# A backward pass of two attention blocks on one core: the second half of q by tokens made during the core loop, and o leaving PSUM by one copy

## The chip, the cores and the metric

The kernel runs on one core of one Trainium2 chip. A core has a matrix engine (TensorE, PE in the profile; its weight loads are PEld), VectorE (DVE), ScalarE (ACT), GpSimd (POOL) and SyncE (SP), which here only issues transfers; 16 DMA engines serve all of them. The metric is the time of one execution on the device in microseconds (us), as the median of several runs.

## The reference

Forward outputs and all gradients are computed in one launch, in bf16, for two attention blocks side by side: block A (linear attention with a feature map) and block B (16 query heads that share one key and one value head, softmax). Sequence length 2048, model width 448, head size 28. The change touches block B alone:

```python
def _B_ref(x, wq, wk, wv, wo):
    B, S, D = x.shape
    H = 16
    Dh = D // H
    q = (x @ wq).reshape(B, S, H, Dh).transpose(0, 2, 1, 3)
    k = x @ wk
    v = x @ wv
    scores = einsum("bhqd,bkd->bhqk", q, k) * (Dh ** -0.5)
    p = softmax(scores, axis=-1)
    o = einsum("bhqk,bkd->bhqd", p, v)
    return o.transpose(0, 2, 1, 3).reshape(B, S, H * Dh) @ wo

out, vjp = jax.vjp(f, A_x, A_wqkv, A_wo, B_x, B_wq, B_wk, B_wv, B_wo)
grads = vjp(grad_out)
```

## The kernel before

The program has three stages. Block A takes the first 190 us. A short stage, `phase_B_pre`, makes q, k and v of block B from about 192 to 221 us. The core, the loop over `u`, makes block B's attention forward and backward at once until about 1030 us, and a tail makes the last weight and input gradients.

**`phase_B_pre`.** For each of 4 groups of 512 tokens (`qc`) it makes q with its channels on the partitions, in `qT` (`R1`): heads are padded to 32 channels, 4 heads to a 128-row slab `g`. Row 0 of each head gets a shift for the softmax, written by four small GpSimd transfers (L580). The core also needs q with its tokens on the rows, in `qn_d` in HBM. After groups 1 and 3, four transposes (L585, by DMA, on SyncE's queue) turn 1024 tokens into `gaT`, and one transfer (L586) stores 1 MB of it.

**The core.** There are 64 blocks `b`, each of 256 queries and two heads, and 8 units `u` to a block, so 512 units; one unit is 256 keys. The order on every engine is written out by hand (`tc.manual_schedule()`). A unit of the stream contains:

- TensorE: the scores S of unit `u` into two of three PSUM banks `SB` (`sps`), and dP = v do of unit `u - 16` into the two banks `DB` (`dps`); in even units o and dq of four earlier units (`o_dq`, into `oq`) and dv (`dv_mm`, into `dv_acc`); in odd units dk (`dk_m`, into `dk_acc`).
- ScalarE: two exponentials, `eT` (L891 and L931), and between them a copy of one half of dP, `cp` (L898).
- VectorE: one half of dS, `dsT` (L896), and a 32 x 32 transpose of an earlier `dsT`, `dsx` (L962).
- GpSimd: the other half of dS (L899).
- SyncE: after every fourth unit one DMA transpose of four units of `eT` into `eN` (L933), 1 MB, which `dv_mm` reads.

Once in a block of 8 units the finished o is handled. At unit 8b + 9, VectorE copies it from `oq` into `oTs` (L913). At 8b + 10, TensorE transposes it with an identity matrix (`onat_T`) into a bank called `spare`, which is the bank of the first S product of the next unit. VectorE then reads it in `o_norm`: the reciprocal of the softmax sum (channel 0, L782) and the scaled o into `oTs` (L783). GpSimd follows with the elementwise product of o and do (`prod`, L787), do divided by the sum (`don`, L790), and a copy of the scaled o over do in `do_nat` (L791). At 8b + 12, `row_D` sums `prod` on VectorE (L795) and GpSimd puts the result into channel 0 of `don` (L796). At 8b + 14, TensorE transposes `don` (`don_T`, L804), which becomes the operand of dP from unit 8b + 16 on.

Every 64 units GpSimd issues the loads of the next `qX` from `qn_d` (L904), 256 KB each and two at a time, at units 38 and 54 of the 64 (the first ones at 10 and 18). It also issues the stores of the output (L711) and one load `wo` (L907, at unit 44). Up to unit 127, `do_proj` makes do from the output gradient and its copies go through VectorE (L866).

A tile of PSUM that one engine reads can be written by TensorE only after that engine has finished; all such waits are semaphores that the framework sets.

Of the kernel before, what the change touches and what calls it, by code (L numbers as in the profile page):

```python
# [9 lines left out]
ALU = mybir.AluOpType  # L10
AX = mybir.AxisListType
BF16 = mybir.dt.bfloat16
F32 = mybir.dt.float32
# [4 lines left out]
P = 128  # L18
# [6 lines left out]
def kernel(  # L25
# [21 lines left out]
    nc = tc.nc  # L47
# [21 lines left out]
    qn_d = dpool.tile([S, 512], BF16, name="qn_d")  # L69
# [9 lines left out]
    def mm(out_ap, lhsT, rhs, start=True, stop=True):  # L79
        nc.tensor.matmul(out_ap, lhsT=lhsT, rhs=rhs, start=start, stop=stop, tile_position=(0, 0))  # L80

    def flat(t):
        return t.rearrange("p a b -> p (a b)")
# [430 lines left out]
    def phase_B_pre(pa, cA, awk, psA, io):  # L514
# [3 lines left out]
        def gen(shape, dt=F32):  # L518
            return psA.tile(shape, dt, name="agen")
# [13 lines left out]
        def k_max(qc, sq):  # L533
            ps = gen([H, 512])
            mm(ps[:, :], ones16[0:32, :], sq[0:32, :])
            nc.vector.tensor_reduce(out=kmx[:, qc:qc + 1], in_=ps[:, :], axis=AX.X, op=ALU.max)

        prev = None
        for qc in range(NQC):
            for w, dst in [(0, kT), (1, vT)]:  # L540
# [7 lines left out]
                else:  # L548
# [4 lines left out]
                                    in1=kT[0:32, qc * 512:(qc + 1) * 512], op=ALU.mult)  # L553
# [5 lines left out]
        for qc in range(NQC):  # L559
            qs = slice(qc * 512, (qc + 1) * 512)  # L560
            pn = psA.tile([P, 512], F32, name="aacc")
            sqs = []
            for g in range(6):
                if qc == 0 and g == 2:
                    k_max(NQC - 1, prev)
                    nc.vector.tensor_reduce(out=kmax2[:], in_=kmx[:], axis=AX.X, op=ALU.max)
                if g < 4:
                    ps = gen([P, 512])
                    for c in range(4):
                        mm(ps[:, :], wq_pad[:, c, g * P:(g + 1) * P], xbT[:, c, qs], start=(c == 0), stop=(c == 3))  # L570
                    nc.scalar.activation(out=qT[:, g, qs], in_=ps[:, :], func=ACT.Copy)
                    sq = awk.tile([P, 512], BF16, name="osb")
                    nc.vector.tensor_tensor(out=sq[:, :], in0=qT[:, g, qs], in1=qT[:, g, qs], op=ALU.mult)
                    sqs.append(sq)
                if g >= 2:
                    mm(pn[:, :], bsel[:, g - 2, :], sqs[g - 2][:, :], start=(g == 2), stop=(g == 5))
            shift = shifts[qc]
            nc.scalar.activation(out=shift, in_=pn[0:H, :], func=ACT.Sqrt, scale=kmax2[:, 0:1])
            for g in range(4):
                nc.gpsimd.dma_start(qT[:, g, qs].rearrange("(j r) s -> j r s", r=32)[:, 0, :], shift[4 * g:4 * g + 4, :])  # L580
            if qc % 2:
                q2 = slice((qc - 1) * 512, (qc + 1) * 512)
                t2 = slice(4 * qc - 4, 4 * qc + 4)
                for g in range(4):
                    nc.sync.dma_start_transpose(qn[:, t2, g * P:(g + 1) * P], qT[:, g, q2])  # L585
                nc.sync.dma_start(qn_d[q2, :].rearrange("(t p) c -> p t c", p=P), qn[:, t2, :])  # L586
# [11 lines left out]
    with ExitStack() as pa:  # L598
        psA = pa.enter_context(tc.tile_pool(name="psA", bufs=4, space=bass.MemoryType.PSUM))
        cA = pa.enter_context(tc.tile_pool(name="cA", bufs=1, side="right"))  # L600
        cB = pa.enter_context(tc.tile_pool(name="cB", bufs=1, side="right"))
        awk = pa.enter_context(tc.tile_pool(name="awk", bufs=3, side="right"))
        io = phase_A(pa, cA, cB, awk, psA)
        phase_B_pre(pa, cA, awk, psA, io)
# [3 lines left out]
    qT_B = [R1[:, g, :] for g in range(4)]  # L608
    vaug, kn, do_nat = vaug_, kn_, R2x[:, 0:NS, :]
    psc = ExitStack()  # L610
    with ExitStack() as cs_:
# [8 lines left out]
        pw_ = cs_.enter_context(tc.tile_pool(name="cwk", bufs=4, side="right"))  # L620
        pp_ = cs_.enter_context(tc.tile_pool(name="cout", bufs=2, side="right"))
# [6 lines left out]
        dsT, dsx, qX, don, doT, rl, prod = ({} for _ in range(7))  # L628
# [13 lines left out]
        def blk(b):  # L642
            qc, pair = divmod(b, 8)
            return qc, pair, pair // 2, pair % 2
# [27 lines left out]
        identF = pp_.tile([P, P], F32, name="identF", bufs=1)  # L672
        make_identity(nc, identF[:])
        oTs = pp_.tile([P, 256], F32, name="oTs", bufs=1)
        wo = pc_.tile([P, 4, D], BF16, name="wo", bufs=1)
        oTq = flat(R4).rearrange("p (t k) -> p t k", k=P)
        W4 = D // 4
        outs = {}
        for m in range(2):
            for n in range(15):  # L680
                q_ = n + (n > 13)
                outs[128 * m + 144 + 8 * n] = (4 * m + q_ // 4, q_ % 4 * W4 - (n == 14) * W4, (q_ % 4 + 1) * W4)
        for n in range(7):
            q_ = n + (n > 5)
# [92 lines left out]
        def o_norm(b):  # L777
            onp = onps.pop(b)
            qc, pair, g, hp = blk(b)
            r_ = pw_.tile([P, 2, 2, 1], F32, name="rl")  # L780
            os_ = oTs[:, 0:P].rearrange("p (q h c) -> p q h c", q=2, h=2)
            nc.vector.reciprocal(out=r_[:], in_=onp[:, :, :, 0:1])  # L782
            nc.vector.tensor_tensor(out=os_, in0=onp[:, :, :, :], in1=r_[:].to_broadcast([P, 2, 2, 32]), op=ALU.mult)  # L783
            rl[b] = r_
            dnv = do_nat[:, 2 * qc:2 * qc + 2, pair * 64:pair * 64 + 64].rearrange("p q (h c) -> p q h c", c=32)
            prod[b] = pw_.tile([P, 2, 2, 32], F32, name="prod", bufs=1)
            nc.gpsimd.tensor_tensor(out=prod[b][:], in0=dnv, in1=os_, op=ALU.mult)  # L787
            dn = pw_.tile([P, 2, 2, 32], BF16, name="don", bufs=3)
            don[b] = dn
            nc.gpsimd.tensor_tensor(out=dn[:], in0=dnv, in1=r_[:].to_broadcast([P, 2, 2, 32]), op=ALU.mult)  # L790
            nc.gpsimd.tensor_copy(out=dnv, in_=os_)  # L791

        def row_D(b):
            Dq = pw_.tile([P, 2, 2, 1], F32, name="Dq")
# [74 lines left out]
        with tc.manual_schedule():  # L869
            tc.keep_in_program_order(nc.scalar.activation(out=ex[:], in_=ex[:], func=ACT.Exp))  # L870
            for u in range(NU + 28):
# [28 lines left out]
                for a in {10: (0, 2), 18: (1, 3)}.get(u, ()) or {38: (0, 2), 54: (1, 3)}.get(u % 64, ()) * (u < 448):  # L900
                    qc = u // 64 + (u > 20)
                    if a == 0:
                        qX[qc] = (pqb_ if qc % 2 else pqa_).tile([P, 4, 2, 512], BF16, name="qX")
                    nc.gpsimd.dma_start(qX[qc][32 * a:32 * a + 32, :, :, :].rearrange("j b s c -> j b (s c)"),  # L904
                                        qn_d[qc * 256:(qc + 1) * 256, :].rearrange("(b j s) c -> j b (s c)", b=4, s=2))
                if u == 44:
                    nc.gpsimd.dma_start(wo, wo_d[:, 0:D].rearrange("(g p) c -> p g c", p=P))  # L907
                if (b := due(u, 12)) is not None:
# [5 lines left out]
                if (b := due(u, 27)) is not None:  # L914
                    qc, pair, g, hp = blk(b)
                    nc.vector.tensor_scalar(out=qT_B[g][64 * hp:64 * hp + 64, qc * 256:(qc + 1) * 256],  # L916
                                            in0=oq[64:128, 0:256], scalar1=scale, scalar2=None, op0=ALU.mult)
                if (b := due(u, 10)) is not None:
                    o_norm(b)
                    if b in (15, 31, 47, 55, 63):  # L920
                        t0, t1 = 2 * (b // 8) - 2 * (b < 48), 2 * (b // 8) + 2
                        nc.sync.dma_start_transpose(oTq[:, 4 * (t0 % 4):4 * (t0 % 4) + 4 * (t1 - t0), :],
                                                    do_nat[:, t0:t1, :].rearrange("p q c -> p (q c)"))
# [12 lines left out]
                if u % 2:  # L936
                    b, i = divmod(u - 27, 8)
# [3 lines left out]
                else:  # L941
                    o_dq((u - 2, u - 1), (u - 20, u - 19))
                    b, n = divmod(u - 20, 8)
# [14 lines left out]
                if 0 <= y < NU:  # L958
                    b, tp = divmod(y, 8)
                    if tp == 0:  # L960
                        dsx[b] = px_.tile([P, 8, 2, 2, 256], BF16, name="dsx")
                    nc.vector.transpose(  # L962
                        out=dsx[b][:, tp, :, :, :].rearrange("p h t c -> p (h t c)").bitcast(F32),
                        in_=dsT[y][:, :, :].rearrange("p h c -> p (h c)").bitcast(F32))
# [16 lines left out]
        for c in range(4):  # L981
            t = dkvT[0:32, :].rearrange("p (t a i) -> p t a i", a=4, i=32)[:, :, c, :]
# [83 lines left out]
```

## Time and profile before

| | |
|---|---|
| median of 13 runs | 1087.62 us |
| lowest and highest | 1082.30 and 1097.21 us |
| the profiled execution | 1097.21 us, span of its instructions 1095.5 us |
| granted TensorE clock, mean of the span | 0.99 |
| busy in the span: PE, DVE, ACT, POOL | 95%, 82%, 80%, 70% |
| bytes moved by DMA | 199.24 MB, of which 175.18 MB on q1, the queue of SyncE |

The profiled execution is the slowest of the 13. In a profile, "idle before, releaser" is the time in which the engine stood before an instruction, and the instruction elsewhere that ended it; "issue" means that nothing in the profile explains the wait. Busy times of VectorE and ScalarE overlap a little at the ends of neighbouring instructions, so the distance between two starts is the better measure of their pace.

### The profile page before, as it was taken

The numbers are of one execution on the slowest core, as the hardware profiler recorded it, in microseconds if no ns is written. First come the engines' busy times: TensorE is split into PE (matmuls) and PEld (weight loads), VectorE is DVE, ScalarE is ACT, GpSimd is POOL, SyncE is SP. The second block draws the span as 40 slices with busy tenths as digits, with TensorE's granted clock in tenths as the row PEclk, the third lists the DMA queues.
The fourth block names the chain that finished last, engine by engine and source line by source line (L and its number), as shares of the span: only waits on it lengthen the run. The fifth ranks groups of instructions, "written<-read, shape, count | busy, mean of one in ns | idle before, by whom it ended". The sixth has DMA issues, their size and how long they took to land.

```text
span 1095.5 us, 41904 instructions
## 1 busy us (share of the span) xinstructions
PE 1041.6 (95%) x17241; PEld 504.6 (46%) x17241; DVE 897.7 (82%) x1790; ACT 874.3 (80%) x1744; POOL 761.9 (70%) x993
## 2 busy tenths in 40 slices
PE   9999999999788999999999999999999999999998
PEld 5545555444343444444444444444444444444444
DVE  7896400439787999999999999999999999999842
ACT  6453122579787999999999999999999999999531
POOL 6001242328776888889889888988988898888840
PEclk9999999989899999999999999999999999999999
DMA  9879899299999999999999999999999999999962
GB/s 241 160 132 190 170 192 216 55 218 198 148 153 189 198 193 187 195 174 202 203 177 186 209 199 181 205 184 187 193 205 187 189 193 197 184 175 180 227 139 64
DMA packets 668384, 199.24 MB, mean 182 GB/s; under 512 B 645408, under 2 KB 664144, under 8 KB 668192
## 3 DMA queue, kind: packets, MB, share of 16 engines
q1 hardware_dynamic: 656320, 175.18, 95.7%
q0 software_dynamic: 6912, 17.43, 7.0%
q10 hardware_dynamic: 4960, 3.96, 1.3%
q8 instruction: 135, 2.21, 0.8%
q14 instruction: 57, 0.47, 0.2%
HBM read 21.00 MB, written 12.94 MB: 31 GB/s over the span
## 4 chain that ended last, share of the span: by engine, by line
PE 34%; ACT 24%; issue 17%; DVE 15%; POOL 8%; DMA 1%; DVEq 0%; ACTq 0%; POOLq 0%; SPq 0%
ACT cp L898 13%; ACT eT L931 10%; PE agen L80 8%; PE sps L639 7%; DVE dsx L962 6%; POOL dsT L899 5%; PE aacc L80 4%; PE oq L639 4%; DVE dsT L896 4%; PE sps L80 4%; PE dk_acc L639 2%; DVE oTs L913 2%; PE dps L639 2%; DVE oTs L783 1%; PE dps L80 1%
## 5 line engine op out<-in xcount | busy, mean ns | idle before, releaser
L899 POOL TENSOR_TENSOR dsT<-cp,eT 128x512 bf16<-128x512 bf16 x512 | 589.1, 1158 | 113.8 <-ACT cp L898 106.1
L639 PEld LDWEIGHTS <-R 128*32 128x32 bf16 (+1 forms) x9184 | 238.2, 94 | 283.2 <-issue 247.9
L896 DVE TENSOR_TENSOR dsT<-dps,eT 128x512 bf16<-128x512 f32 x512 | 342.0, 668 | 26.2 <-PE dps L639 20.9
L962 DVE STREAM_TRANSPOSE dsx<-dsT 128x512 f32<-128x512 f32 x512 | 357.7, 699 | 2.4 <-DVE ot L709 0.2
L891 ACT ACTIVATE eT<-sps 128x512 bf16<-128x512 f32 x512 | 312.9, 611 | 36.1 <-PE dps L639 22.1
L898 ACT ACTIVATE cp<-dps 128x512 bf16<-128x512 f32 x512 | 314.5, 614 | 12.0 <-PE dps L639 10.5
L931 ACT ACTIVATE eT<-sps 128x512 bf16<-128x512 f32 x512 | 320.7, 626 | 0.0
L639 PE MATMUL dk_acc<-dsx,qX 32*32 32x512 bf16 x4096 | 270.2, 378 | 3.8 <-issue 3.8
L639 PE MATMUL dps<-doT,R 32*128 32x256 bf16 x2048 | 247.6, 270 | 2.4 <-DVE dsT L896 0.7
L639 PE MATMUL sps<-R,R 32*128 32x256 bf16 (+1 forms) x2240 | 224.0, 276 | 10.4 <-DVE R L866 1.7
L639 PE MATMUL oq<-dsT,R 128*32 128x256 bf16 x2048 | 157.7, 275 | 6.9 <-issue 6.8
L639 PE MATMUL oq<-eT,R 128*32 128x256 bf16 x2048 | 159.3, 276 | 1.0 <-issue 1.0
L639 PEld LDWEIGHTS <-qX 32*32 32x32 bf16 x4096 | 80.2, 89 | 118.9 <-issue 59.1
L639 PE MATMUL dv_acc<-eN,don 128*32 128x512 bf16 x1024 | 98.0, 381 | 0.0
L80 PEld LDWEIGHTS <-R 128*128 128x128 bf16 (+1 forms) x525 | 41.4, 99 | 42.0 <-issue 15.0
L400 POOL COPY pk<-R 128x256 bf16<-128x256 bf16 x4 | 1.6, 398 | 73.8 <-DVE R L360 73.7
L552 DVE TENSOR_TENSOR osb<-R 32x512 bf16<-32x512 bf16 x4 | 1.7, 413 | 59.0 <-ACT R L549 59.0
L639 PE MATMUL sps<-identF,oTs 128*32 128x64 f32 x1024 | 27.9, 225 | 7.9 <-issue 0.4
L639 PEld LDWEIGHTS <-don 128*32 128x32 bf16 x1024 | 34.8, 98 | 0.5
L787 POOL TENSOR_TENSOR prod<-R,oTs 128x128 f32<-128x128 bf16 x64 | 27.7, 433 | 8.2 <-DVE oTs L783 8.2
L916 DVE TENSOR_SCALAR R<-oq 64x256 bf16<-64x256 f32 x64 | 27.3, 427 | 4.4 <-PE oq L639 2.4
L80 PE MATMUL agen<-R,R 128*128 128x448 bf16 x128 | 28.6, 352 | 0.8 <-ACT R L219 0.6
(223 smaller groups left out, 986.8 us busy)
## 6 DMA issues: line engine op xcount, KB each, us to landing
qX<-qn_d POOLq DMA_DIRECT2D x32, 256.0 KB, 4.7
out_dram<-osb ACTq DMA_DIRECT2D x22, 112.0 KB
qn_d<-gaT SPq DMA_DIRECT2D x2, 1024.0 KB
eN<-eT SPq DMA_TRANSPOSE x128
xa<-in_A_x_dram SPq DMA_DIRECT2D x8, 224.0 KB
ga<-in_grad_out_dram SPq DMA_DIRECT2D x4, 448.0 KB
xa<-in_grad_out_dram POOLq DMA_DIRECT2D x4, 448.0 KB, 8.9
out_dram<-wdq POOLq DMA_DIRECT2D x8, 224.0 KB, 4.4
```

The source lines that it names most:

```text
L80: nc.tensor.matmul(out_ap, lhsT=lhsT, rhs=rhs, start=start, stop=stop, tile_position=(0, 0))
L639: nc.tensor.matmul(out, lhsT=lhsT, rhs=rhs, start=start, stop=stop, tile_position=pos, skip_group_check=True)
L783: nc.vector.tensor_tensor(out=os_, in0=onp[:, :, :, :], in1=r_[:].to_broadcast([P, 2, 2, 32]), op=ALU.mult)
L787: nc.gpsimd.tensor_tensor(out=prod[b][:], in0=dnv, in1=os_, op=ALU.mult)
L891: nc.scalar.activation(out=eT(u)[:, 0, :], in_=sp[0][:, :], func=ACT.Exp, scale=scale)
L896: nc.vector.tensor_tensor(out=dst[:, 0, :], in0=dp[0][:, :], in1=ew[:, 0, :], op=ALU.mult)
L898: nc.scalar.activation(out=cp[:, :], in_=dp[1][:, :], func=ACT.Copy)
L899: nc.gpsimd.tensor_tensor(out=dst[:, 1, :], in0=cp[:, :], in1=ew[:, 1, :], op=ALU.mult)
L913: nc.vector.tensor_copy(out=oTs[0:64, :], in_=oq[0:64, 0:256])
L916: nc.vector.tensor_scalar(out=qT_B[g][64 * hp:64 * hp + 64, qc * 256:(qc + 1) * 256], in0=oq[64:128, 0:256], scalar1=scale, scalar2=None, ...
L931: nc.scalar.activation(out=eT(u)[:, 1, :], in_=sp[1][:, :], func=ACT.Exp, scale=scale)
L962: nc.vector.transpose(out=dsx[b][:, tp, :, :, :].rearrange("p h t c -> p (h t c)").bitcast(F32), in_=dsT[y][:, :, :].rearrange("p h c -> p ...
```

## The change

It has two parts. First, `phase_B_pre` makes only the first half of q by tokens (`if qc == 1`). The second half, blocks 4 to 7 of 256 queries, is made during the core: at units 122, 186, 250 and 314 four DMA transposes on SyncE's queue bring one block of 256 tokens into a new tile `qS`, and 10 units later two GpSimd transfers store it in `qn_d`. Second, `o_norm` copies the whole o from PSUM to `oTs` without scaling and takes the reciprocal from that copy. GpSimd now makes `don` first, `prod` from `don` and the unscaled o, and the scaled o for `do_nat` by a product in place of the copy.

```diff
-            if qc % 2:
+            if qc == 1:
                 q2 = slice((qc - 1) * 512, (qc + 1) * 512)
                 t2 = slice(4 * qc - 4, 4 * qc + 4)
                 for g in range(4):
                     nc.sync.dma_start_transpose(qn[:, t2, g * P:(g + 1) * P], qT[:, g, q2])
...
+        qS = pp_.tile([P, 8, P], BF16, name="qS", bufs=1)
...
             os_ = oTs[:, 0:P].rearrange("p (q h c) -> p q h c", q=2, h=2)
-            nc.vector.reciprocal(out=r_[:], in_=onp[:, :, :, 0:1])
-            nc.vector.tensor_tensor(out=os_, in0=onp[:, :, :, :], in1=r_[:].to_broadcast([P, 2, 2, 32]), op=ALU.mult)
+            nc.vector.tensor_copy(out=os_, in_=onp[:, :, :, :])
+            nc.vector.reciprocal(out=r_[:], in_=os_[:, :, :, 0:1])
             rl[b] = r_
             dnv = do_nat[:, 2 * qc:2 * qc + 2, pair * 64:pair * 64 + 64].rearrange("p q (h c) -> p q h c", c=32)
-            prod[b] = pw_.tile([P, 2, 2, 32], F32, name="prod", bufs=1)
-            nc.gpsimd.tensor_tensor(out=prod[b][:], in0=dnv, in1=os_, op=ALU.mult)
             dn = pw_.tile([P, 2, 2, 32], BF16, name="don", bufs=3)
             don[b] = dn
             nc.gpsimd.tensor_tensor(out=dn[:], in0=dnv, in1=r_[:].to_broadcast([P, 2, 2, 32]), op=ALU.mult)
-            nc.gpsimd.tensor_copy(out=dnv, in_=os_)
+            prod[b] = pw_.tile([P, 2, 2, 32], F32, name="prod", bufs=1)
+            nc.gpsimd.tensor_tensor(out=prod[b][:], in0=dn[:], in1=os_, op=ALU.mult)
+            nc.gpsimd.tensor_tensor(out=dnv, in0=os_, in1=r_[:].to_broadcast([P, 2, 2, 32]), op=ALU.mult)
...
+                if u in (122, 186, 250, 314):
+                    q_ = u // 64 + 3
+                    for g_ in range(4):
+                        nc.sync.dma_start_transpose(qS[:, 2 * g_:2 * g_ + 2, :], qT_B[g_][:, q_ * 256:(q_ + 1) * 256])
+                if u in (132, 196, 260, 324):
+                    q_ = u // 64 + 2
+                    for t in range(2):
+                        nc.gpsimd.dma_start(
+                            qn_d[q_ * 256 + t * P:q_ * 256 + (t + 1) * P, :].rearrange("p (g c) -> p g c", c=P),
+                            qS[:, :, :].rearrange("p (g t) c -> p t g c", t=2)[:, t, :, :])
                 if u == 44:
                     nc.gpsimd.dma_start(wo, wo_d[:, 0:D].rearrange("(g p) c -> p g c", p=P))
                 if (b := due(u, 12)) is not None:
                     row_D(b)
```

## The prediction

> **What bounds the kernel now.** I read the windows first (which stretches run off pace), then the SyncE queue and TensorE's waits in the slow ones, then the timelines of one undisturbed block of 8 units. Columns of a window: PE, PEld, DVE, ACT and POOL busy, granted clock, DMA share, GB/s.
>
> ```profile
> 280.00:300.00 20.00, 14.47 (x282) 6.53 (x276) 13.87 (x28) 13.88 (x29) 13.58 (x17) 0.88 1.25 131
> 300.00:320.00 20.00, 17.08 (x320) 7.44 (x312) 15.11 (x28) 15.12 (x31) 13.47 (x16) 0.86 1.27 171
> 320.00:340.00 20.00, 15.77 (x308) 7.16 (x304) 14.66 (x30) 14.52 (x29) 12.34 (x15) 0.91 1.19 157
> 340.00:360.00 20.00, 19.20 (x387) 9.09 (x388) 19.38 (x38) 19.65 (x40) 17.29 (x22) 1.00 1.16 195
> ...
> 600.00:620.00 20.00, 19.20 (x420) 9.53 (x416) 19.65 (x40) 19.88 (x41) 17.96 (x22) 1.00 1.27 190
> ```
>
> In the core ScalarE is busy 19.9 of 20 us, VectorE 19.7, TensorE 19.2, GpSimd 18.0: four engines nearly full, so what counts is the waits on the path between them. Undisturbed, a block takes 12.05 us (starts of L782, 438 to 788 us), 12.35 while `do_proj` runs. But 280 to 340 us runs at three quarters of that pace with half-clock stretches: the three blocks from 286.4 to 339.1 us take 52.6 us where 3 x 12.35 = 37.0 are due. 15.6 us are lost there. What TensorE waited for:
>
> ```profile
> 297.34 0.40 PE L639 MATMUL oq<-dsT,R 128*32 128x256 bf16 x2 [4.55 <-issue]
> ...
> 307.80 0.29 PE L639 MATMUL oq<-dsT,R 128*32 128x256 bf16 x2 [2.25 <-issue]
> ...
> 332.57 1.65 PE L639 MATMUL dk_acc<-dsx,qX 32*32 32x512 bf16 x15 [3.79 <-issue]
> ```
>
> 10.6 us are idle and charged to no engine ("issue"), the rest is the half clock behind them. In the trace's DMA packets the 16 KB instruction pieces of queue q8, otherwise mostly 6 us apart, come late just here (282.2, 293.6, 305.4 and 317.6, 329.9 us), so I read them as late instruction fetches. The Trainium skill, "Runtime: NRT & Kernel Launch", section Instruction fetch mechanics, says that instructions arrive by DMA in blocks of that size. The `qX` loads are late too: 10.2 to 14.9 us to landing between 275 and 325 us, 3.4 to 5.6 from 380 us on. Why it is crowded is on the SyncE queue:
>
> ```profile
> 222.89 7.72 SPq L585 DMA_TRANSPOSE gaT<-R  x4
> 230.72 7.79 SPq L933 DMA_TRANSPOSE eN<-eT  x1
> 238.68 0.46 SPq L586 DMA_DIRECT2D qn_d<-gaT  x1
> 239.19 66.25 SPq L933 DMA_TRANSPOSE eN<-eT  x9
> ```
>
> The second half of q takes 7.7 us there for its transposes and stores 1 MB at 238.7, while the first `eN` transposes are already due. One is due every 6.0 us and takes 5.2 to 5.5: only 0.6 to 0.8 us is caught up each time. Against the ends of L931, L933 is 2.7 us late at the first, 8.8 at the fifth, 16.6 at 305 us, and on time only from 379 us.
>
> **The change, part by part.** The sum is against the profiled execution's own 1097.21 us (span 1095.5 and 1.7 around it); the median of 13 is 1087.62, the fastest 1082.30.
>
> (1) Second half of q leaves the entry. Off SyncE's queue go 4 transposes (7.7 us) and the 1 MB store; L933 then starts on time at about 228 us and stays within some 2 us of it. Nothing else waits there: until 245 us TensorE is the pace (its do_proj and S products, partly at half clock), so at the entry itself I count 0. The gain is the 15.6 us, if the crowding makes them. 1097.2 - 15.6 = 1081.6 is close to the fastest run, so an execution without these stalls exists; the median one has lost 1087.6 - 1081.6 = 6.0 to them. Value: all of it; bounds 0 and 15.6 against the own time (0 and 6.0 against the median).
>
> (2) `o_norm`, 64 times. Now reciprocal, then scaling, both from PSUM; then the bank `spare` is free for the next unit's S product.
>
> ```profile
> 643.52 0.18 DVE L782 RECIPROCAL rl<-sps 128x4 f32<-128x4 f32 x1
> 643.74 0.29 DVE L783 TENSOR_TENSOR oTs<-sps,rl 128x128 f32<-128x128 f32 x1
> ...
> 643.64 0.40 PE L639 MATMUL dv_acc<-eN,don 128*32 128x512 bf16 x4
> 644.09 0.28 PE L639 MATMUL sps<-R,R 32*128 32x256 bf16 x2
> ...
> 643.72 0.65 ACT L931 ACTIVATE eT<-sps 128x512 bf16<-128x512 f32 x1
> 644.50 0.60 ACT L891 ACTIVATE eT<-sps 128x512 bf16<-128x512 f32 x1
> ```
>
> S starts 0.06 after L783 ends, ScalarE 0.41 after S: its pitch is 0.78 here where 0.48 is usual. The copy comes first afterwards: about 0.28 us (the 64x256 copy L913 takes 405 ns, the 112-column cast L709 272), so the bank is free 0.22 earlier. TensorE uses only part: S follows the last dv_acc by 0.424 us in 59 blocks, and by 0.311 at least where nothing holds it. That leaves 0.113, of which ScalarE sees 0.10, since in those cases exp follows S by 0.424, not 0.410. 59 x 0.10 = 5.9 us gained. Bounds 0 (another wait takes its place) and 59 x 0.113 = 6.7. VectorE's own work is the same: 0.18 + 0.29 before, 0.28 and a reciprocal of 0.15 to 0.18 from SBUF after, which now waits for the copy as the scaling waited for the reciprocal. What queues behind it is L962, at an unchanged time.
>
> (3) GpSimd scales, 64 times. The nearest rows:
>
> ```profile
> L787 POOL TENSOR_TENSOR prod<-R,oTs 128x128 f32<-128x128 bf16 x64 | 27.7, 433 | 8.2 <-DVE oTs L783 8.2
> ...
> L791 POOL CAST R<-oTs 128x128 bf16<-128x128 f32 x64 | 18.6, 291 | 4.1
> ```
>
> The cast becomes a product of about 433: +0.14 us each, 9 us of work (bounds 0.11 from the 400 of L790, and 0.3 if two f32 inputs are dearer). GpSimd waits about 0.31 us for ScalarE in most units, which hides it; without that cover it costs the 9. `don` must be ready for TensorE's L804 two units later: there 0.43 to 0.54 us lie between the end of L796 and L804, which starts behind L931. In 4 blocks after qX issues (499 to 788 us) only 0.13 to 0.15 lie there, of which 0.05 is the hand-over, and near 254 us nothing: 4 x 0.05 + 0.14, about 0.3 us lost. `prod` comes 0.45 later, still before L795 needs it.
>
> (4) In the core, at units 122, 186, 250, 314: 4 transposes on SyncE's queue. Nearest row: 4-block ones (L103) 1.19 to 1.27 us, so 4.9 us; L933 is then some 4 late and catches up in five or six groups. eN is read 17 units after its first group, so 0 on the path. At 132, 196, 260, 324, 2 stores on GpSimd's queue, ahead of L796, in pieces of 256 B: 512 each. Nearest row for such an issue, at the same place in a block, is `wo`:
>
> ```profile
> 291.28 0.80 POOL L907 DMA_DIRECT2D wo<-wo_d  x1
> 292.10 0.23 POOL L796 TENSOR_TENSOR don<-Dq,rl 128x4 bf16<-128x4 f32 x1
> ...
> 254.99 0.23 PE L804 MATMUL sps<-identB,don 128*32 128x128 bf16 x2 [0.86 <-POOL don L796]
> ```
>
> The last line shows the price when `don` is late: TensorE stands, and what is queued behind L804 (o, dq, dv, the next S) with it. Two issues are 1.6 us, with the 0.14 of (3) 1.74, less the 0.53 of slack in these blocks: 1.2 us, four times, 4.8 us lost. Bounds 0 (short issues) and 4 x 1.7. The stores also wait for the transposes: issued by unit 126 or 127 and landed about 2 us on, some 6 us before unit 132; without that margin the whole GpSimd queue stands, dsT first. qX reads the stores 34 units later.
>
> Here a rule is weighed. After the 2.25 us stall the clock was at one half from 309.0 to 312.4 us. The Trainium skill, "TensorE: Matmul & The Clock Gate", Part 1, has it fall only after an idle window of about 3.4 us. By the 2.25 us row a 1.2 us stall might add 1.7 us each, 6.8 in all; by the rule nothing. After the 0.86 us stall of 254 us the clock stayed at 1.00. That row is nearer, so I take nothing and keep the 6.8 for the range.
>
> Sum: 1097.2 - 15.6 - 5.9 + 0.3 + 4.8 = 1080.8; from the median, 1087.6 - 6.0 - 5.9 + 0.3 + 4.8 gives the same. I say 1081.
>
> **The rivals.** *The stalls have another cause.* At 250 us L933 was 7 to 8 us late, two qX loads ran, and TensorE lost little; the slow windows also have DMA stretches of a few GB/s. If the disturbance is from outside, it stays: 1087.6 - 5.9 + 0.3 + 4.8 = 1086.8, no change.
> *The crowding moves into the core* (slower). At the four places L933 is some 4 us late just as 256 KB are stored in 1,024 small pieces. If TensorE's fetch is then late as at 293 us, a place costs 15.6 / 3 = 5.2 us: all four 1081 + 21 = 1102, two of them 1091.5. It decides from two places on. For it: the same mixture stood at 282 us. Against it: L922 made L933 2.3 and 3.2 us late at 443 and 637 us, without a stall.
> *The S product gains nothing*, because the work ahead of it moves later by as much: with relief 1081.6 + 0.3 + 4.8 = 1086.7, without it 1092.7. Against it: the 0.113 stands in 59 of 61 blocks.
>
> **How the numbers follow.** Relief at the entry with the small sums: 0.57, mostly 1076 to 1084. No relief, or nothing from S: 0.24, about 1087. Crowding in the core: 0.19, 1091 and more. About 0.3% (3.3 us) is what a measurement of this kernel can tell from no change, so the three are faster, same and slower, some of the first lying in "same" and some of the second in "faster". The range goes from the first without the store stalls (1080.8 - 4.8 and with the full 6.7 of (2): 1075.2) to two crowded places (1091.5).
>
> **What would show it.** Right: L933 on time from the first groups, qX landing in about 5 us at units 38 and 54, no idle "issue" of over 2 us near 290 us, S 0.31 us after dv_acc at `o_norm`, ScalarE's pitch 0.67, and four waits of about 1.2 us of L804 for GpSimd. Wrong: stalls near 290 us although L933 is on time; stalls near the four stores; L804 late in most blocks; a pitch still 0.78.

## The result, and the profile after

The changed kernel takes 1108.16 us (median of 11 runs, 1096.44 to 1123.21), the kernel before 1086.37 us beside it: a ratio of 1.0179, 95% interval 1.0152 to 1.0207. It is slower by 1.8%, about 19.4 us, where 1081 and thus a gain of some 6 us was predicted. The ratios leave out runs that are over 1.5% above the fastest of their kernel (three of these 11), so this one is below the quotient of the medians, 1.020. The profiled execution has a span of 1101.7 us. The execution of before that the prediction read (1097.2 us) was one of the longest of its kernel, so the terms below are compared as ratios of runs, not between the two profiles.

The line numbers of a profile are those of its own kernel, so the same instruction stands a few lines further down in some runs. First the windows of the changed kernel, in the columns of before: busy PE, PEld, DVE, ACT, POOL, granted clock, DMA share, GB/s.

```profile
280.00:300.00 20.00, 18.49 (x396) 8.78 (x399) 18.74 (x37) 18.88 (x38) 17.61 (x20) 1.00 1.24 211
300.00:320.00 20.00, 19.25 (x396) 9.24 (x392) 19.39 (x37) 19.77 (x41) 18.49 (x24) 1.00 1.14 204
320.00:340.00 20.00, 19.15 (x411) 8.94 (x404) 19.28 (x40) 19.49 (x39) 16.75 (x21) 1.00 0.99 169
...
420.00:440.00 20.00, 18.24 (x369) 7.93 (x368) 18.26 (x36) 18.89 (x39) 17.96 (x22) 1.00 1.12 196
480.00:500.00 20.00, 15.97 (x303) 6.80 (x306) 14.57 (x29) 14.56 (x30) 13.62 (x16) 0.83 1.19 183
720.00:740.00 20.00, 16.17 (x303) 6.86 (x300) 14.36 (x29) 14.77 (x30) 14.09 (x17) 0.83 0.96 167
```

The three windows that were slow before now run at full pace and full clock: the relief at the entry came. But 480 to 500 and 720 to 740 us, where the kernel before was undisturbed, look as 280 to 340 did: a quarter of the work missing, clock 0.83. The slow stretches have moved. What TensorE waited for there (its timeline; in brackets the idle time before and what ended it):

```profile
429.10 0.23 PE L805 MATMUL sps<-identB,don 128*32 128x128 bf16 x2 [1.25 <-POOL don L797]
490.87 0.40 PE L639 MATMUL dps<-doT,R 32*128 32x256 bf16 x2 [3.73 <-issue]
733.00 0.29 PE L805 MATMUL sps<-identB,don 128*32 128x128 bf16 x2 [3.44 <-POOL don L797]
798.85 0.29 PE L639 MATMUL oq<-dsT,R 128*32 128x256 bf16 x2 [3.46 <-issue]
...
427.35 1.45 POOL L914 DMA_DIRECT2D qn_d<-qS  x2
731.23 1.48 POOL L914 DMA_DIRECT2D qn_d<-qS  x2 [2.17 <-issue]
```

The first is the predicted stall behind two stores (1.2 us forecast). The second and the fourth are "issue" stalls, each with half clock behind it (489.1 to 495.9 and 799.7 to 803.1 us), nowhere near a store: they come at units 173 and 366, a few units after a pair of `qX` loads. At the third GpSimd itself had stood for 2.17 us in front of its two stores, whose transposes were late (the last two rows: the stores of the first and of the fourth place); half clock follows there too, from 731.4 to 738.2 us. The SyncE queue around the first set, that is the four transposes of one block of q (L944 makes `eN`, one for each group of four units; L910 is new, L933 is the transpose of o, `oTq`), and the exponential that completes the group of the second L944 row:

```profile
405.74 7.09 SPq L944 DMA_TRANSPOSE eN<-eT  x1
412.88 6.92 SPq L910 DMA_TRANSPOSE qS<-R  x4
419.90 10.59 SPq L944 DMA_TRANSPOSE eN<-eT  x2
430.60 3.54 SPq L933 DMA_TRANSPOSE R<-R  x1
434.24 70.90 SPq L944 DMA_TRANSPOSE eN<-eT  x12
...
411.42 0.60 ACT L942 ACTIVATE eT<-sps 128x512 bf16<-128x512 f32 x1
```

The four transposes took 6.9 us, not 4.9. From here I measure lateness as the start of an L944 against the end of the L942 that completes its four units. After the set it is 7.9 us (419.90 - 412.02), after L933 9.4 us, and it then falls by only about 0.5 us a group: a late L944 starts 5.54 us after the one before it (median), and one is due every 6.02. Where a pair of `qX` loads lands, an L944 takes 10.5 us (at 483.4) and the lateness jumps back to 8.0; it drops to 1.9 only because the core itself then stands. It is still 1.2 us when the second set makes it 8.6, and it peaks at 15.4 us at 730 us. In the kernel before it was over 4 us nowhere after 379 us. The `qX` loads show it (last number: median us from issue to landing; before it was 4.7):

```profile
qX<-qn_d POOLq DMA_DIRECT2D x32, 256.0 KB, 6.9
```

### The profile page after: what moved, and what is told of

It is laid out like the page before. It is cut to its first block, busy times and chain, and to the rows that moved or that the text cites. A ratio compares the mean times of both kernels' runs of the same rounds, so it can differ in the third digit from the quotient of the medians.

```text
span 1101.7 us, 41931 instructions
## 1 busy us (share of the span) xinstructions
PE 1040.4 (94%) x17241; PEld 495.5 (45%) x17241; DVE 896.4 (81%) x1790; ACT 878.1 (80%) x1744; POOL 771.8 (70%) x1001
## 3 DMA queue, kind: packets, MB, share of 16 engines
q8 instruction: 135, 2.21, 0.8%
## 4 chain that ended last, share of the span: by engine, by line
PE 46%; ACT 25%; issue 11%; DVE 11%; POOL 5%; DMA 1%; SPq 0%; ACTq 0%; DVEq 0%; POOLq 0%
ACT cp L899 13%; PE agen L80 13%; ACT eT L942 10%; PE sps L639 9%; PE oq L639 6%; PE aacc L80 4%; DVE dsT L897 4%; PE sps L80 4%; DVE dsx L973 3%; POOL dsT L900 3%; PE dps L639 2%; PE dk_acc L639 2%; PE dv_acc L639 2%; ACT eT L892 2%; PE dps L80 1%
## 5 line engine op out<-in xcount | busy, mean ns | idle before, releaser
L639 PEld LDWEIGHTS <-R 128*32 128x32 bf16 (+1 forms) x9184 | 230.4, 94 | 293.7 <-issue 257.0
L942 ACT ACTIVATE eT<-sps 128x512 bf16<-128x512 f32 x512 | 319.4, 624 | 0.0
L805 PE MATMUL sps<-identB,don 128*32 128x128 bf16 x256 | 18.7, 224 | 16.1 <-POOL don L797 10.0
L789 POOL TENSOR_TENSOR don<-R,rl 128x128 bf16<-128x128 bf16 x64 | 26.0, 406 | 8.8 <-DVE rl L784 8.8
L791 POOL TENSOR_TENSOR prod<-don,oTs 128x128 f32<-128x128 bf16 x64 | 27.5, 430 | 5.0
```

Of the source, the lines that this page charges most:

```text
L639: nc.tensor.matmul(out, lhsT=lhsT, rhs=rhs, start=start, stop=stop, tile_position=pos, skip_group_check=True)
L791: nc.gpsimd.tensor_tensor(out=prod[b][:], in0=dn[:], in1=os_, op=ALU.mult)
L805: nc.tensor.transpose(tp2[q:q + 32, qb * P:(qb + 1) * P], don[b][:, qb, h, :], identB[:, :], tile_position=(0, q))
L942: nc.scalar.activation(out=eT(u)[:, 1, :], in_=sp[1][:, :], func=ACT.Exp, scale=scale)
```

## The experiments

Theory A: the transposes make SyncE's queue late for hundreds of microseconds, and `qX` loads and instruction fetches suffer. Theory B: the stores stop GpSimd, and with it TensorE. Rival C: the new `o_norm` loads GpSimd. Ratios are to the kernel before, run on the same chip in the same batch.

### Taking the in-core work apart: e1, e2, e3, e4

e1 deletes both new `if u in (...)` parts; the loads of the last four q blocks get rows that exist:

```diff
-                if u in (122, 186, 250, 314):  ... 4 transposes
-                if u in (132, 196, 260, 324):  ... 2 stores
-                  qn_d[qc * 256:(qc + 1) * 256, :]
+                  qn_d[qc % 4 * 256:(qc % 4 + 1) * 256, :]
```

> The changed kernel without its in-core transposes and stores: the second half of q by tokens is never made, and the qX loads of the last four q blocks read the first four instead (same sizes). Theory A (SyncE's queue stays late from unit 122 on): all of the loss is in what is left out here; the entry's relief (6 us of the median) and the new o_norm (2.5 us by the block period of the changed kernel's trace) remain, so about 1078 us. Theory B (the stores stop GpSimd and with it TensorE): the same 1078. Rival C (the new o_norm loads GpSimd, don comes late): the loss stays, about 1100 or more. If the entry's relief is worth nothing: 1084.

Measured: 1081.25 us, ratio 0.9950 (0.9927 to 0.9973). Without the second half of q the kernel is faster than before, so the whole loss is in that work, and rival C falls. But the gain is 5.4 us (0.5%), where entry relief and `o_norm` together were predicted at 11.9, and the time is above the 1078 expected.

e2 keeps the transposes and drops the stores:

```diff
-                if u in (132, 196, 260, 324):  ... 2 stores
```

> The changed kernel with its 16 in-core transposes but without the 8 stores: the second half of q by tokens is made and not used, the qX loads of the last four q blocks read the first four (same sizes). Theory A (the transposes make SyncE's queue late for some 450 us; qX loads and instruction fetches come late, TensorE stands): nearly the whole loss, 1098 to 1108 us. Theory B (the stores): about 1078 to 1082, with L944 as late as in the changed kernel but no stalls. The prediction's step 4 priced this part at 0, which would give about 1078.

Measured: 1102.22 us, ratio 1.0139 (1.0108 to 1.0170). The 16 transposes, whose results nobody reads, cost 1.89% against e1, 20.6 us. What TensorE waited for in it (total, times, longest us):

```profile
PE oq L639 <- issue: 6.2, 5, 4.0
PE dv_acc L639 <- DMA eN<-eT: 3.9, 1, 3.9
PE dps L639 <- issue: 3.4, 2, 3.1
PE dk_acc L639 <- issue: 2.1, 2, 1.8
PE sps L805 <- POOL don L797: 2.0, 4, 0.8
```

No wait for a store is left (the 2.0 us for `don` are in e1 too, 2.2), and the "issue" stalls are still there: 3.10 us at unit 173 and 3.99 at unit 252. In the trace's DMA packets the instruction pieces of q8, mostly 6 us apart, have gaps of 11.0 us (475.0 to 486.0) and 13.3 us (599.1 to 612.4) at these two. The second line is a new kind: at 740.8 us `eN` itself came too late for `dv_acc`, with these transposes 13 us behind. Block by block (starts of the reciprocal), four of e2's 64 blocks, at 483, 609, 688 and 738 us, take 18.8 us longer than in e1, of 22.2 us for the whole core in the two profiles. They are the blocks of the stalls over 1.5 us; the loss is there, not at the four places of the sets.

What ends the "issue" stalls can be read as well. The 135 pieces of q8 are TensorE's, about 255 of its 34,482 matmuls and weight loads to a piece. At the first stall:

```profile
478.26 1.12 POOL L905 DMA_DIRECT2D qX<-qn_d  x2
...
489.29 0.39 PE L639 MATMUL dps<-doT,R 32*128 32x256 bf16 x2 [3.10 <-issue]
```

The late piece, begun at 486.0, ended at 487.9, and TensorE went on at 489.3. The 13 traces have 21 "issue" stalls of over 1.7 us between 240 and 1030 us. In each of them a piece ended inside the stall, in 18 of them 1.3 to 1.8 us before TensorE went on (in the others 2.1, 2.9 and 3.1). So these are waits for instructions; a wait of TensorE for `qX` itself stands in none of the traces.

e3 keeps the stores and drops the transposes:

```diff
-                if u in (122, 186, 250, 314):  ... 4 transposes
+        nc.gpsimd.memset(qS[:], 1.0)      # once, ahead of the core
```

> The changed kernel with its 8 stores but without the 16 transposes: what is stored is a constant set once, so the second half of q by tokens is wrong. Theory A: only the direct stalls of TensorE for don, 4 x 1.25 us, come on top of 1078: about 1083 us, L944 on time nearly everywhere. Theory B (256-byte pieces crowd the queues or the GpSimd issues do the harm): most of the loss, 1095 us or more, with the stalls near 487 and 795 us still there.

Measured: 1087.20 us, ratio 1.0000 (0.9980 to 1.0021); against e1 0.50%, 5.4 us.

```profile
PE sps L806 <- POOL don L798: 7.9, 9, 1.3
```

That is e1's 2.2 us and, for the rest, mainly four stalls of 1.22 to 1.25 us behind the four pairs of stores. L944 is never over 3.4 us late and no "issue" wait exceeds 1.1 us. The small pieces of the stores, 256 B each, do no harm beyond the time of their issue. Theory B is right for a quarter of the loss, theory A has the rest.

e4 is the changed kernel with the `o_norm` of before:

> The changed kernel with the o_norm of before: only the move of q's second half into the core. Theories A and B: the new o_norm brings about 2.5 us, so this is 1110 us. The prediction's step 2 (5.9 us): 1114. Rival C (the new o_norm causes the loss): 1080 to 1090.

Measured: 1113.81 us, ratio 1.0230 (1.0207 to 1.0252). It is slower than the changed kernel's 1.0179, so the new `o_norm` helps; the difference of 0.5% has the uncertainty of both. The 1114 of step 2 was hit, but e5 does not bear step 2 out.

The terms add up: 20.6 for the transposes, 5.4 for the stores, less e1's 5.4, are 20.6 us; measured are 19.4.

### What the new `o_norm` brings: e5

The kernel before with the diff's part in `o_norm` alone.

> The kernel before with the new o_norm alone. By the difference of the changed kernel and the one with the old o_norm (1113.8 - 1108.2) and by the prediction's step 2: -5.7 to -5.9, about 1082 us. By the block period of the traces (12.09/12.01 against 12.05/11.96 us, so 0.045 us a block): -2.6, about 1085 us.

Measured: 1084.45 us, ratio 0.9979 (0.9956 to 1.0002), a gain of 2.3 us that is at the edge of what can be told from none; it agrees with the block period and is less than half of the forecast. The traces show where the rest went. The pitch of ScalarE's exponentials, from start to start, is 0.776 us at `o_norm` before, 0.681 in e5 and 0.676 in the changed kernel: the 0.10 us that were forecast. But two units later ScalarE waits longer than before. In the medians of blocks 16 to 59 (before and e5) the unit at 8b + 12 grows from 1.593 to 1.653 us in one kind of block and from 1.478 to 1.527 in the other. One block of e10 (below, the same `o_norm`; L891, L932: exponentials; L896: `dsT`):

```profile
642.95 0.65 ACT L932 ACTIVATE eT<-sps 128x512 bf16<-128x512 f32 x1
643.62 0.60 ACT L891 ACTIVATE eT<-sps 128x512 bf16<-128x512 f32 x1
...
646.03 0.64 ACT L932 ACTIVATE eT<-sps 128x512 bf16<-128x512 f32 x1
646.72 0.60 ACT L891 ACTIVATE eT<-sps 128x512 bf16<-128x512 f32 x1
...
645.65 0.69 DVE L896 TENSOR_TENSOR dsT<-dps,eT 128x512 bf16<-128x512 f32 x1
...
646.39 0.28 PE L639 MATMUL dps<-doT,R 32*128 32x256 bf16 x2
646.40 0.28 PE L639 MATMUL sps<-R,R 32*128 32x256 bf16 x2
```

and the same place of a block before:

```profile
655.73 0.66 ACT L931 ACTIVATE eT<-sps 128x512 bf16<-128x512 f32 x1
656.50 0.60 ACT L891 ACTIVATE eT<-sps 128x512 bf16<-128x512 f32 x1
...
658.91 0.64 ACT L931 ACTIVATE eT<-sps 128x512 bf16<-128x512 f32 x1
659.54 0.60 ACT L891 ACTIVATE eT<-sps 128x512 bf16<-128x512 f32 x1
```

0.67 us lie between the first two where it was 0.77, and 0.69 between the next two where it was 0.63. At 646.39 dP starts 0.05 us after L896 has ended (645.65 + 0.69), and the second S product is queued behind it. VectorE has no gap of more than 0.05 us from the copy at 642.74 to that L896, 2.91 us later; in the block of before the same stretch, from the reciprocal at 655.53 to L896 at 658.47, was 2.94 us. So, as I read it, with TensorE's wait gone VectorE is next, and of 0.10 us about half is given back; no run tested this by itself. The sum of the eight pitches falls from 12.076 to 12.036 and from 12.020 to 11.981 us: 0.04 us a block, an estimate of 2.4 us for 60 blocks.

### Is it the burst, or the work? e6 and e7

e6 issues the same transposes 12 units apart, and the stores 16 units after the last of a set:

```diff
-                if u in (122, 186, 250, 314):
+                r_ = u - 122
+                if 0 <= r_ < 256 and r_ % 64 in (0, 12, 24, 36):  # one transpose
-                if u in (132, 196, 260, 324):
+                if u in (174, 238, 302, 366):
```

> The changed kernel with the same 16 transposes 12 units (18 us) apart, not four at once, and the stores of a q block at units 174, 238, 302, 366 (mod 8 = 6, sixteen units after the last transpose, and midway between two pairs of qX loads). Theory A (SyncE's lateness adds up): each transpose of 1.2 us is caught up in two or three eN groups, L944 is never over some 3 us late except behind the oTq transpose, no stall over 2 us: 1081 us plus 0 to 6 for the stores, 1081 to 1087. If the work itself costs (DMA time of 16 transposes, wherever they stand): 1100 or more.

Measured: 1098.53 us, ratio 1.0109 (1.0074 to 1.0145). Better than the burst by 0.7%, but my forecast of 1081 to 1087 fell. SyncE's queue tells why:

```profile
434.66 1.24 SPq L910 DMA_TRANSPOSE qS<-R  x1
436.00 16.61 SPq L944 DMA_TRANSPOSE eN<-eT  x3
452.67 1.25 SPq L910 DMA_TRANSPOSE qS<-R  x1
454.02 16.16 SPq L944 DMA_TRANSPOSE eN<-eT  x3
```

From one L910 to the next are 18.01 us, and three groups are due every 3 x 6.02 = 18.06: with one small transpose to three groups the queue is exactly full, nothing is caught up, and L933 and the `qX` loads come on top. L944 stays 1 to 12 us late from 415 to 965 us. I had counted with an `eN` transpose of 4.9 us. That is a short one: in e1 those of a queue on time take 5.38 us in the median, and here the late ones take 5.53.

e7 also moves the stores to SyncE's queue (`nc.sync.dma_start`, the two of a set 8 units apart).

> As the spread version, and the stores go by SyncE's queue, the two of a block 8 units apart. Theory A and the store stalls of 6 us both: 1080 to 1083 us, no wait of L805 for don over 1 us. If 512 pieces of 256 B on SyncE's queue hold the eN transposes as the burst did: 1090 or more.

Measured: 1107.70 us, ratio 1.0211 (1.0173 to 1.0250), worse than e6. A store takes 0.58 to 0.63 us on SyncE, small beside GpSimd's stall, but the queue had nothing left: the `eN` transposes are up to 13.5 us late, and TensorE waited for `eN` up to 4.6 us. The `don` waits are down to 0.8 us at the longest, as forecast; that part seems to be worth less than the room on SyncE.

### Late queue alone, or late queue and a load? e8

The kernel of e2, without the `qX` loads from unit 64 on; the products read the first two tiles again:

```diff
-  {38: (0, 2), 54: (1, 3)}.get(u % 64, ()) * (u < 448)
+  {38: (0, 2), 54: (1, 3)}.get(u % 64, ()) * (u < 64)
-  qX[qc]  (in dk_m)
+  qX[qc % 2]
```

> The kernel with transposes only, and without the qX loads from unit 64 on (the products that read qX take the first two q blocks' tiles again; same instructions, same sizes). Is a late SyncE queue enough for the stalls, or does it take a qX load that lands on top of it? Late queue enough: stalls near 487, 611, 741 us stay, 1095 us or more. Both needed: L944 is as late as with the loads (8 to 13 us), and the stalls over 2 us are gone: 1078 to 1084 us.

Measured: 1079.31 us, ratio 0.9934 (0.9912 to 0.9955). About 22 us (2%) below e2. On SyncE the same work as in e2 stands at the same places:

```profile
410.30 7.03 SPq L910 DMA_TRANSPOSE qS<-R  x4
417.43 10.59 SPq L938 DMA_TRANSPOSE eN<-eT  x2
428.12 3.12 SPq L927 DMA_TRANSPOSE R<-R  x1
431.34 76.98 SPq L938 DMA_TRANSPOSE eN<-eT  x14
508.38 6.03 SPq L910 DMA_TRANSPOSE qS<-R  x4
```

and the lateness behind a set is 5.0 to 6.7 us, up to 7.8 after the transpose of o. This is less than the 8 to 13 us expected, and than the 13.6 us that e2 reaches with the loads. Between 400 and 1000 us the longest wait of TensorE is 0.4 us. One window of e2, then the same of e8:

```profile
480.00:500.00 20.00, 16.49 (x312) 6.94 (x311) 14.98 (x29) 15.15 (x32) 13.78 (x16) 0.83 1.16 183
```

```profile
480.00:500.00 20.00, 19.34 (x411) 9.18 (x408) 19.68 (x40) 19.90 (x41) 17.83 (x23) 1.00 1.23 191
```

So a queue up to 7.8 us late costs nothing that shows here; the 13 us at which e2 waited for `eN` do not occur. For the "issue" stalls it takes a `qX` load that lands on top: in e2 the load issued at 478.8 us took 12.3 us to land and the stall came at 486.2; the queue was then 4.0 us late, and this load made it 7.8. In e1 the same load meets a queue on time and lands in 4.9 us. Without loads the lateness of a set is gone after 11 or 12 groups (6.7 at 514 us, 0.4 at 574, nothing at 580), so a set also no longer starts on what the last one left. A kernel with neither transposes nor loads was not run; with waits of 0.4 us at most it could show little.

### The same reading on the kernel before: e9, e10

If a load on a late queue makes the stalls, those near 290 us in the kernel before should go when nothing but the two pairs of loads there is moved:

```diff
-  {10: (0, 2), 18: (1, 3)}.get(u, ()) or {38: (0, 2), 54: (1, 3)}.get(u % 64, ()) * (u < 448)
+  {10: (0, 2), 18: (1, 3), 62: (0, 2), 78: (1, 3)}.get(u, ()) or
+      {38: (0, 2), 54: (1, 3)}.get(u % 64, ()) * (64 < u < 448)
```

> The kernel before, q's second half still made at the core's entry, with one thing moved: the qX loads of the second q block at units 62 and 78, not 38 and 54 (they are needed from unit 91). If the stalls near 290 us are made by qX loads that land on a late SyncE queue, as in the kernel with transposes only, they go although SyncE has as much to do at the entry: 1081 to 1084 us against 1087.6, L933 back on time by about 320 us and not 379. If SyncE's lateness alone, or something else, makes them: 1087 to 1088, no change.

Measured: 1083.45 us, ratio 0.9956 (0.9939 to 0.9972), a gain of 4.8 us by moving two pairs of issues. The blocks between 286 and 339 us take 12.3 to 12.7 us each. One part of the forecast missed: in the profiled execution, the longest of the 17, the `eN` transposes were not on time by 320 us, but 3 to 11 us late until about 460, and a stall of 4.47 us stood at 416 us, again at a `qX` load that took 10.4 us to land. So a load on a late queue does not always make a stall: those of 319 and 344 us met a queue 3 to 4 us late and took 7.6 to 10.8 us without one.

> The same with the new o_norm: another 3 us (as the new o_norm alone brought), so about 1078 to 1081 us, faster than both kernels; 1084 if moving the loads does nothing.

Measured: 1082.64 us, ratio 0.9947 (0.9925 to 0.9969). It beats the kernel before by 5.8 us and the changed kernel by 2.3%. The forecast of 1078 to 1081 was missed: over e9 the new `o_norm` brings 0.1%, less than the uncertainty. In its profile the entry is clean:

```profile
280.00:300.00 20.00, 18.42 (x389) 8.84 (x380) 18.72 (x37) 19.23 (x39) 17.42 (x21) 1.00 1.22 218
300.00:320.00 20.00, 19.30 (x394) 8.62 (x387) 19.27 (x39) 19.20 (x40) 16.84 (x20) 1.00 1.00 179
320.00:340.00 20.00, 18.92 (x412) 9.52 (x408) 19.28 (x37) 19.52 (x41) 17.54 (x21) 1.00 1.15 205
```

### Sets where the queue has time: e11

The four sets at units 58, 186, 314 and 378, the stores 10 units behind each; three of them do not meet L933.

> The changed kernel with the four sets of transposes at units 58, 186, 314, 378 (the stores 10 units behind each), so that three of the four do not meet the oTq transpose of units 130 and 258 and start from a queue that is on time; the next qX load is 44 units (66 us) later. Late queue and qX load together make the stalls: 6 us of lateness at 0.55 us a group is down to about 0.5 when the load comes, so no stall over 2 us there; what remains is one set (378) of some 5 us and the stores' 6 us: 1086 to 1094 us. If each set costs its 5 us wherever it stands: 1100 to 1108.

Measured: 1097.65 us, ratio 1.0072 (1.0047 to 1.0098). By the ratio that is 7.8 us above before and at the upper end of the forecast; by the medians of all runs it is 11.0 and beyond it. The runs spread from 1086.5 to 1108.8 us. In the profiled execution, one of the longest, the first set behaved as forecast: 5.5 us late behind it, on time nine groups later, the next loads landing in 3.7 to 5.6 us, no stall but the store's 1.26 us. Behind the second the queue was 7.7 us late, still 1.7 and 4.0 at the next two pairs of loads, one of these took 14.3 us, and a stall of 3.95 us followed. The third and the fourth brought a wait of 3.60 us for `don`, one of 2.21 for `eN` and "issue" stalls of 3.66 and 3.22. Distance helps, but 44 units are not enough, and I read the spread of the runs as the small differences in what is left when the load comes; that was not tested by itself.

## Why the prediction was wrong, point by point

| step | predicted, us | measured |
|---|---|---|
| (1) relief at the entry, from the median | -6.0 | e1 less e5: -0.29%, -3.2 us (uncertain by about as much) |
| (2) `o_norm` | -5.9 | e5: -2.3; by the pitch 60 x 0.04 = -2.4 |
| (3) GpSimd's product | +0.3 | not measured by itself; L792 takes 0.402 us against 0.291 of the copy |
| (4) transposes | 0 | e2 less e1: +1.89%, +20.6 us |
| (4) stores | +4.8 | e3 less e1: +0.50%, +5.4 us |

**The step that failed is (4), "L933 is then some 4 late and catches up in five or six groups ... so 0 on the path".** It put the transposes at 0; they cost 20.6 us. Three things in it were wrong. The set took 6.9 us, behind an `eN` transpose that had itself taken 7.1, so L944 was 7.9 us late, not 4. (That transpose is as long in e1, 7.05 at 408 us: the pair of `qX` loads of unit 118 lands during it.) The queue catches up 0.5 us a group, not 0.7, so it takes 12 groups and more, and the next set and L933 come before it is done. And the path was sought in the wrong reader: `eN` is indeed read late enough nearly always (TensorE waited for it once in e2), but a `qX` load, issued 44 units after the set, finds the queue late, and TensorE's instructions come late with it. The prediction had both facts in hand, 0.6 to 0.8 us caught up each time and stalls at the entry with `qX` landing late, and put them together for the kernel before only. The cover that it named (17 units until `eN` is read) was no cover for the loads and the instruction pieces, which go through the same 16 DMA engines.

**The rival that hit.** "The crowding moves into the core" put a place at 5.2 us and all four at 1102. That e2 has 20.6 / 4 = 5.2 us and 1102.2 is in part luck: e2 is without the stores, which the 1102 included, and the changed kernel took 1108. What does agree is the price of one stall with its half clock: three of e2's four long blocks lose 5.2 to 6.3 us. The places do not: they are late loads, not the four stores. Its evidence for (256 KB in 1,024 pieces) was wrong: e2 has none of these stores, and in e3 they make no "issue" stall of over 1.1 us. Its evidence against was wrong too: L922 had made L933 2.3 and 3.2 us late without a stall because, as I read it, the next `qX` load came 36 units later, when the queue was on time again. It was given too little.

**What held.** Step (1) in its mechanism: L944 starts on time at the entry, at most 1.7 us late up to unit 119, and the stalls near 290 us are gone; only the size is about half. e9 shows that they need the loads: with the store and the four transposes in place, and the queue still 3 to 6 us late between 286 and 339 us, they are gone when the loads come later. Step (2) in its first half: S follows dv by 0.311 us, pitch 0.68; the bound of 0, "another wait takes its place", was half true. Step (4) for the stores: 1.25 us each at the first three places; the fourth waited 3.44 us because the transposes were late, where 6 us of margin had been claimed. And the clock: behind the stalls of 1.25 us it stayed at 1.00 (the window from 420 to 440 us), as the prediction took it. The rule weighed there, an idle window of about 3.4 us, is nevertheless too strict for this kernel: the stall of 3.73 us began at 487.1 us and half clock at 489.1.

## What to carry to other kernels

A queue's free time is the interval at which its work is due less the distance at which that work starts when it is already behind: here 6.02 - 5.5 = 0.5 us a group. Divide the added work by that (a set of 6 to 7 us takes 12 to 14 groups), and ask which transfers start before the debt is paid. A transfer that "has 17 units until it is read" still made the `qX` loads land late in this kernel, and with them TensorE's instructions. Before work is moved off a crowded place, look whether one small transfer there can be moved instead: two pairs of load issues, 24 units later, gave 4.8 us, where 6.0 at the entry were hoped of the whole move.

## What was not expected of the hardware

- A DMA transpose of 1 MB on a queue that is on time mostly takes 4.8 to 5.5 us, and up to 7.2 while `qX` loads land (e1, 430 to 960 us, median 5.38 of 54); in a late queue the median is 5.47 (e2, 85 of them). What a queue can catch up is not seen in the shortest one.
- Transposes of two 128 x 128 blocks took 1.24 us in the median (1.20 to 2.5), about what four blocks take (medians 1.22 to 1.27 us); eight blocks (L585) took 1.23 to 2.64, median 1.43. Four of the small ones together took between 5.6 and 7.0 us in e8.
- The clock did not follow the length of a stall. None of the stalls of 1.25 us lowered it (e3 has no half clock from 240 us to the end of the loop). In e6 a stall of 1.38 us at 811.0 was followed by half clock from 813.3 us, and one of 2.28 us at 655.7 by none. It went by fixed windows: in each trace all changes of the clock from 220 us on stand whole multiples of 3.413 us apart, to within 2 ns. All 22 windows of that grid (at full clock, 240 to 1030 us) in which TensorE was busy for less than half were followed by half clock. Between half and two thirds it went both ways (14 followed by half clock, 17 not), and above that it happened once in some 2,900.
- All 21 "issue" stalls of TensorE over 1.7 us held the end of a late instruction piece of q8, mostly 10 to 13 us behind the one before. Not every gap makes a stall: e8 has one of 10.5 us (510.3 to 520.8) without. And not every stall has the same partners: that of 305.6 us in the kernel before began 9 us after the loads had landed, on a queue 16.6 us late, and one of 2.08 us in e4 (300.9 us) had neither a load nor a late queue. How a late transpose queue together with a load keeps the fetch back was not seen in the traces and stays open.
